# Pooled scores in two banks, local outputs by column halves, and small products in the gaps behind the first tile

## The chip, the core and the metric

One core of a Trainium2 chip runs the whole program. The engines are TensorE (PE; its weight loads are listed apart as PEld), VectorE (DVE), ScalarE (ACT), GpSimd (POOL) and SyncE (SP), which issues transfers. Each works through its own instructions in order, and semaphores tie them together. The metric is the device time of one execution in microseconds; lower is better. TensorE has two clock levels, 1.2 and 2.4 GHz; the profile gives the granted clock as a share of the upper one, so that 0.50 is the lower.

## What is computed

An attention layer over 4 batches, 8 heads, 576 positions and 64 dimensions, then two feed-forward layers on its 2304 tokens of 512 features. The attention has two branches that are added: one on positions pooled by four, and one in which each query sees only keys less than four positions away.

```python
q_d = q.reshape(B, H, Sd, factor, D).mean(axis=3)      # factor 4; k_d, v_d alike
out_up = np.repeat(sm_attn(q_d, k_d, v_d), factor, axis=2)
mask = np.abs(pos[:, None] - pos[None, :]) < factor
scores = np.where(mask, scale * np.matmul(q, k.transpose(0, 1, 3, 2)), -1000000000.0)
out_local = np.matmul(softmax(scores), v)
x = (out_up + out_local)                               # as [2304, 512]
h = x @ w_in;  x = (h * sigmoid(h)) @ w_out            # first layer, hidden size 2048
h = x @ w_in2; out = elu(h) @ w_out2                   # second layer
```

(softmax stands for the lines with the maximum, the exponential and the sum.)

## The kernel before

The 16 pairs of a batch and two heads are the units of the attention; the two heads of a pair lie in the two halves of 64 partitions. The first layer starts long before the attention is done: its tokens are cut into tiles of 256, its hidden features into tiles of 128, and `unit(n, f)` makes, for token tile n and hidden tile f, the first product (L1160, 12 matmuls, 128x256), the activation (ACT L1188, DVE L1189, ACT L1191, POOL L1194) and the second product (L1208, 12 matmuls). Each number of a product is split into a high and a low part and three of the four partial products are taken, so a weight tile has two parts too: DVE L466 and ACT L459 and L462 decode it, ACT L1137 rounds the high part, POOL L1141 makes the low part. From about 257 us on, the rest of the feed-forward work runs in another phase (`paired`, L1842 to L1999), which the change doesn't touch.

A pair passes PE in these steps: transposes of queries and keys (L674), local scores (L811: 20 matmuls of 64 columns on tiles of 64x64 of the array, for batch 0 with a mask product, L803, ahead), pooled scores (L884: six matmuls of 144 columns, `pooled_scores`, for three groups of pooled queries and two heads, the heads on the tiles at rows and columns 0 and 64), flips of the local weights (L928) and of the pooled weights (L950), pooled output (L975) and local outputs (L1041, `out_l`: 20 matmuls of about 57 columns, on four tiles of 64x64). Between the pooled scores and L950 stand the maximum (DVE L894), three exponentials (ACT L900), sums (DVE L908, L909) and a norm (POOL L915). L822 on POOL is the same norm for the local weights. L936 and L962 copy the flips from the banks.

PSUM is eight banks, `b0` to `b7`, handed out by `banks`: kind "h" for a first product's tile (it uses the left half of a bank), "y" for the second product's sums, "a" for the attention. A `Hold` is a bank that is taken when its first step is issued and given back after its last user.

The order of all engines' instructions up to about 257 us is made by a list scheduler while the program is built: every step is a `Job` with an engine, an assumed time, predecessors, holds and a due time. `pick` takes the job that can start earliest, and among those that can start within `SLACK` the one due first; on PE a job with the same tile size (`mode`) as the last one is preferred (`STICK`). So a changed number or hold moves the whole sequence. Until the first unit's first product is out (`FILL_TO`), `fill` puts products of a constant tile (L389, 512 columns) where the planner foresees that PE would stand still.

## Time and profile before

| | us |
| --- | --- |
| median of 3 runs | 859.21 |
| lowest, highest | 858.85, 860.39 |
| the profiled execution | 860.57 |
| its span in the profile | 858.8 |

| engine | busy us | share of the span |
| --- | --- | --- |
| PE | 849.1 | 99% |
| DVE | 679.0 | 79% |
| ACT | 566.9 | 66% |
| POOL | 197.2 | 23% |

The mean granted clock of PE is 0.996. The profile is of one execution. Matmuls are pipelined on PE, and the ends of their records are modelled, so the distance between the starts of two rows tells more than the duration in a row. A row of the timeline groups records of one line that follow each other; a matmul in fp32 shows as two records.

### The profile page before, as it was taken

The numbers are of one execution on the slowest core, as the hardware profiler recorded it, in microseconds if no ns is written. First come the engines' busy times: TensorE is split into PE (matmuls) and PEld (weight loads), VectorE is DVE, ScalarE is ACT, GpSimd is POOL, SyncE is SP. The second block draws the span as 40 slices with busy tenths as digits, with TensorE's granted clock in tenths as the row PEclk, the third lists the DMA queues.
The fourth block names the chain that finished last, engine by engine and source line by source line (L and its number), as shares of the span: only waits on it lengthen the run. The fifth ranks groups of instructions, "written<-read, shape, count | busy, mean of one in ns | idle before, by whom it ended". The sixth has DMA issues, their size and how long they took to land.

```text
span 858.8 us, 18415 instructions
## 1 busy us (share of the span) xinstructions
PE 849.1 (99%) x7032; PEld 817.6 (95%) x7032; DVE 679.0 (79%) x1360; ACT 566.9 (66%) x1316; POOL 197.2 (23%) x239
## 2 busy tenths in 40 slices
PE   9989999999999999999999999999999999999998
PEld 6878999999999999999999998899998999999997
DVE  6987776766947988967969889569889999487495
ACT  4877765655549876655478597377499885473662
POOL 6676785754000300000000111000020102002010
PEclk9989999999999999999999999999999999999999
DMA  9686977621065255033188466163586670561602
GB/s 174 167 191 172 179 187 192 154 65 78 27 168 178 81 195 160 1 129 93 64 243 286 168 238 229 65 230 105 188 285 221 209 268 15 199 207 38 229 29 74
DMA packets 120056, 132.66 MB, mean 154 GB/s; under 512 B 64992, under 2 KB 96224, under 8 KB 119840
## 3 DMA queue, kind: packets, MB, share of 16 engines
q1 hardware_dynamic: 117600, 130.90, 50.1%
q8 instruction: 55, 0.90, 0.5%
q10 hardware_dynamic: 2368, 0.59, 0.4%
q14 instruction: 33, 0.27, 0.1%
HBM read 89.26 MB, written 42.21 MB: 153 GB/s over the span
## 4 chain that ended last, share of the span: by engine, by line
PE 96%; DVE 2%; issue 1%; DMA 0%; ACT 0%; POOL 0%; DVEq 0%; SPq 0%; POOLq 0%
PE b L1894 34%; PE b L1844 14%; PE b L1208 8%; PE b L1997 8%; PE b L1999 8%; PE b L1160 7%; PE b L1842 7%; PE b L674 2%; PE b L884 1%; PE b L1041 1%; PE b L975 1%; PE b L811 1%; PE b L950 1%; PE b L928 1%; PE b L747 1%
## 5 line engine op out<-in xcount | busy, mean ns | idle before, releaser
L1160 PE MATMUL b<-xh,w 128*128 128x256 f32 x384 | 82.7, 296 | 0.0
L1208 PE MATMUL b<-gh,w 128*128 128x256 f32 x384 | 79.5, 289 | 0.0
L1894 PE MATMUL b<-xhr,xaw 128*128 128x384 f32 x288 | 77.3, 335 | 0.0
L1894 PE MATMUL b<-xhr,w 128*128 128x384 f32 x256 | 67.3, 334 | 0.0
L1160 PEld LDWEIGHTS b<-xh,w 128*128 128x128 f32 x384 | 64.8, 195 | 2.3 <-issue 1.4
L1208 PEld LDWEIGHTS b<-gh,w 128*128 128x128 f32 x384 | 62.9, 190 | 1.3 <-issue 0.8
L1906 ACT COPY hg<-b 128x384 f32<-128x384 f32 x60 | 28.9, 482 | 43.2 <-PE b L1894 42.8
L1804 DVE TENSOR_TENSOR part<-b,part 128x256 f32<-128x256 f32 (+3 forms) x91 | 41.1, 500 | 18.8 <-PE b L1844 17.8
L1902 DVE TENSOR_TENSOR b<-b,hg 128x384 f32<-128x384 f32 x60 | 33.5, 561 | 27.8 <-PE b L1894 17.2
L1208 PE MATMUL b<-gl,w 128*128 128x256 f32 x192 | 54.3, 283 | 0.0
L1894 PE MATMUL b<-xlr,xaw 128*128 128x384 f32 x160 | 53.5, 334 | 0.0
L1894 PEld LDWEIGHTS b<-xhr,xaw 128*128 128x128 f32 x288 | 52.4, 188 | 0.0
L1334 DVE TENSOR_TENSOR xlr<-tail,xhr 128x768 fp32r<-128x768 f32 x42 | 40.0, 954 | 14.8 <-ACT xhr L1331 14.6
L1160 PE MATMUL b<-xl,w 128*128 128x256 f32 x192 | 49.8, 286 | 0.0
L1997 PE MATMUL b<-grw,w 128*128 128x384 f32 x192 | 49.6, 334 | 0.0
L1894 PEld LDWEIGHTS b<-xhr,w 128*128 128x128 f32 x256 | 46.5, 188 | 0.0
L1331 ACT CAST xhr<-tail 128x768 fp32r<-128x768 f32 x42 | 35.5, 847 | 12.1 <-DVE tail L1506 11.2
L1894 PE MATMUL b<-xlr,w 128*128 128x384 f32 x128 | 42.8, 334 | 0.0
L1844 PE MATMUL b<-w,grw 128*128 128x256 f32 x228 | 42.6, 283 | 0.0
L1999 PE MATMUL b<-w,grw 128*128 128x512 f32 x132 | 41.6, 389 | 0.0
L822 POOL TENSOR_TENSOR ring<-ring,small 128x640 f32<-128x640 f32 x27 | 34.3, 1272 | 23.1 <-DVE small L854 14.1
L1333 POOL TENSOR_TENSOR ghk<-hg,grw 128x384 fp32r<-128x384 f32 x4 | 4.5, 1132 | 151.8 <-ACT grw L1331 151.8
(376 smaller groups left out, 2834.2 us busy)
## 6 DMA issues: line engine op xcount, KB each, us to landing
ws<-in_moe_w_in_dram SPq DMA_DIRECT2D x30, 512.0 KB, 5.5
ws<-in_moe_w_out_dram SPq DMA_DIRECT2D x30, 512.0 KB, 4.5
tailr<-xs SPq DMA_DIRECT2D x28, 384.0 KB, 4.3
xs<-xhr SPq DMA_DIRECT2D x21, 384.0 KB, 2.3
xs<-xlr SPq DMA_DIRECT2D x21, 384.0 KB, 2.8
x<-part SPq DMA_DIRECT2D x6, 768.0 KB, 3.8
tail<-x SPq DMA_DIRECT2D x12, 384.0 KB, 5.9
out_dram<-part SPq DMA_DIRECT2D x18, 256.0 KB, 2.0
```

Of the source, the lines that this page charges most:

```text
L822: eng.tensor_tensor(E3(s0, s1), E3(s0, s1), col3(h, s0, s1).to_broadcast([P, 2 * (s1 - s0), WIN]), op)
L1160: nc.tensor.matmul(ph.tile[:, :NB0], w[a][:, c, :], x_slot(n, c, b_), start=start and m == 0, stop=stop and m == len(products) - 1,)
L1208: nc.tensor.matmul(y[d // 2].tile[:, o:o + NB0], w[m // 2][:, sl], gg(m % 2), start=f == 0 and m == 0 and d % 2 == 0, stop=fin and m == 2, ...
L1331: a = Job("A", ACT_[width], lambda: nc.scalar.copy(hi(), at()), preds, gate)
L1334: other=("V", VEC_[width], lambda: nc.vector.tensor_tensor(lo(), at(), hi().bitcast(F32), ALU.subtract)),
L1804: nc.vector.tensor_tensor(dst, x, dst, ALU.add)
L1842: nc.tensor.matmul(y, wm[:, sl], gm, start=first, stop=last_, skip_group_check=True)
L1844: nc.tensor.matmul(y, gm[:, sl], wm, start=first, stop=last_, skip_group_check=True)
L1894: nc.tensor.matmul(acc_, a[:, cs], b[:, c, :], start=fresh and c == 0 and m == 0, stop=c == 1 and m == 2, skip_group_check=True,)
L1902: add = lambda out, x, y: Job("V", VEC_[NB], lambda: nc.vector.tensor_tensor(out, x, y, ALU.add), [], gate)
L1997: nc.tensor.matmul(y[d][:, :NB], wm[:, sl], gm, start=first, stop=last_)
L1999: nc.tensor.matmul(y[d], gm[:, sl], wm, start=first, stop=last_)
```

## The change

Three edits.

The pooled scores get two banks instead of one (`bankd`, `group_d`): groups 0 and 2 in the first, group 1 in the second. The six matmuls are issued so that the two heads' tiles write to the two banks in the first and third round. The maximum becomes two instructions, over two groups (288 elements) and one (144), the exponentials come in the order 0, 2, 1, and the planner's time for the block goes from 0.4 to 0.5.

The local outputs' 20 matmuls are issued in another order: first the ten whose results go to partitions 0 to 63 of the two banks, then the ten for partitions 64 to 127; within ten, the row halves and the banks take turns.

`fill_beside` goes on where `fill` ends, until the fourth hidden tile of the second token tile has its first product (`SOFT_TO`): where the planner foresees that PE would stand still by more than 0.3 us plus 0.115 us, it puts products of the mask tile (bf16, 256 columns, adding onto the unused right half of a bank that a first product holds). 25 such products come about.

```diff
--- before.py
+++ after.py
@@ -62,6 +62,7 @@
     POOL_G = 1
     D_ROWS, D_LOCAL, D_V, D_W, S_ROWS, S_LOCAL, X_AFTER = 1.6, 2.3, 1.75, 2.5, 1.1, 2.2, 1
     QUAD_FROM, MASK_PE = 0, 1
+    SOFT_TO = (1, FP // 2 - 1)
     FILL_TO, SAFE_R, SAFE_W = (0, 0), 0.0, 0.0
     LEND = 1
     SOON, W_EARLY, W_AT = 10.0, 0, -3.0
@@ -94,7 +95,7 @@
     QD = [a * SD // 3 for a in range(3)]
     QD_ROWS = (D, SD // 3)
     QD_FROM = ([min(a, SD - D) for a in QD], QD)
-    T_D = 0.4
+    T_D = 0.5
 
     LENT = {'rows': [(6, 0), (6, 1)], 'v': [(7, 1)]}
 
@@ -163,7 +164,7 @@
     now = [0.0]
     trim = [True]
     clock_of = {"A": 0.0, "V": 7.0, "G": 7.0, "S": 0.0, "P": 5.0, "dma": 0.0, "port": 7.0}
-    filling = [True]
+    filling, soft = [True], [True]
     serial = [0]
     mode_of = [None]
 
@@ -296,6 +297,8 @@
             if self.eng == "P":
                 if filling[0]:
                     fill(t)
+                elif soft[0]:
+                    fill_beside(t)
                 if self.mode != mode_of[0]:
                     dur += 0.12 if mode_of[0] is not None else 0.09
                 mode_of[0] = self.mode
@@ -392,6 +395,15 @@
         gap = t - clock_of["P"]
         filler(min(int((gap - 0.1) / 0.22), 40))
 
+    def fill_beside(t):
+        gap = t - clock_of["P"]
+        n = min(int((gap - 0.3) / 0.115), 40)
+        beside = [h for h in banks.busy.values() if h.kind == "h" and h.left > 0]
+        flat = masks.rearrange("p a s w -> p (a s w)")
+        if n > 0 and beside:
+            for _ in range(n):
+                nc.tensor.matmul(beside[0].tile[:, NB0:2 * NB0], flat[:, :P], flat[:, :NB0], start=False, stop=False, skip_group_check=True)
+
     wz = []
     fill_bank = Hold(banks, "f")
     fill_bank.left = 1
@@ -874,34 +886,41 @@
             )
 
 
-            bankd = Hold(banks, "a")
-
-            def pooled_scores(bankd=bankd):
+            bankd = [Hold(banks, "a") for _ in range(2)]
+
+            def group_d(a, bankd=bankd):
+                return bankd[a % 2].tile[:, a // 2 * SD:(a // 2 + 1) * SD]
+
+            def pooled_scores(group_d=group_d):
                 qD, kD = hqkD.tile, hqkD.tile[:, SD:]
-                for a in range(3):
-                    for j in range(2):
-                        c0, m = QD_FROM[j][a], D
-                        nc.tensor.matmul(
-                            bankd.tile[j * D:j * D + m, a * SD:(a + 1) * SD], qD[j * D:(j + 1) * D, c0:c0 + m], kD[j * D:(j + 1) * D, :],
-                            start=True, stop=True, skip_group_check=True,
-                        )
-
-            psd = follow(Job("P", T_D, pooled_scores, [red], lat=0.2, takes=[bankd, hsm] + [hED] * (b >= POOL_G), uses=[hqkD], mode="q"), "psd")
+                for j, a in ((0, 0), (1, 1), (0, 2), (1, 0), (0, 1), (1, 2)):
+                    c0 = QD_FROM[j][a]
+                    nc.tensor.matmul(
+                        group_d(a)[j * D:(j + 1) * D], qD[j * D:(j + 1) * D, c0:c0 + D], kD[j * D:(j + 1) * D, :],
+                        start=True, stop=True, skip_group_check=True,
+                    )
+
+            psd = follow(Job("P", T_D, pooled_scores, [red], lat=0.2, takes=bankd + [hsm] + [hED] * (b >= POOL_G), uses=[hqkD], mode="q"), "psd")
             hnm = Hold(NM)
             DP = D + QD_ROWS[1]
-            bank3d = lambda bankd=bankd: bankd.tile[:DP, :3 * SD].rearrange("p (a s) -> p a s", a=3)
-            nmj = Job(
-                "V", 0.14 + 0.00106 * SD * 3, lambda: nc.vector.tensor_reduce(hnm.tile[:DP, :3], bank3d(), axis=AX.X, op=ALU.max, negate=True),
-                [psd], takes=[hnm],
-            )
-
-            def exp_d():
-                for a in range(3):
+            nmj = []
+            for o in range(2):
+                na = 2 - o
+
+                def top_d(o=o, na=na, bankd=bankd):
+                    nc.vector.tensor_reduce(
+                        hnm.tile[:DP, o:3:2], bankd[o].tile[:DP, :na * SD].rearrange("p (a s) -> p a s", a=na), axis=AX.X, op=ALU.max, negate=True,
+                    )
+
+                nmj.append(Job("V", 0.14 + 0.00106 * SD * na, top_d, [psd] + nmj, takes=[] if o else [hnm]))
+
+            def exp_d(group_d=group_d):
+                for a in (0, 2, 1):
                     nc.scalar.activation(
-                        ED()[:DP, a, :], bank3d()[:, a, :], AF.Exp, bias=hnm.tile[:DP, a:a + 1], accum_out=hsm.tile[:DP, 2 * a:2 * a + 1],
+                        ED()[:DP, a, :], group_d(a)[:DP], AF.Exp, bias=hnm.tile[:DP, a:a + 1], accum_out=hsm.tile[:DP, 2 * a:2 * a + 1],
                     )
 
-            exps = [Job("A", 0.58 * 3, exp_d, [nmj], uses=[hnm, bankd])]
+            exps = [Job("A", 0.58 * 3, exp_d, nmj, uses=[hnm] + bankd)]
             mine = lambda: hnm.tile[:DP, :3]
 
             def invert():
@@ -1030,16 +1049,16 @@
 
             def out_l(banko=banko):
                 vw = hw.tile.rearrange("p (n d) -> p n d", d=D)
-                for i_ in range(NW // 2):
-                    for t in range(2):
-                        w = i_ + t * NW // 2
-                        n = a0[w + 1] - a0[w]
-                        c0 = (w % 2) * WIN + a0[w] - q0[w]
-                        o = a0[w] - t * HALF
-                        for j in range(2):
-                            p_ = (j + t) % 2 * D
+                for e in range(2):
+                    for i_ in range(NW // 2):
+                        for t in range(2):
+                            w = i_ + t * NW // 2
+                            n = a0[w + 1] - a0[w]
+                            c0 = (w % 2) * WIN + a0[w] - q0[w]
+                            o = a0[w] - t * HALF
+                            j = t ^ e
                             nc.tensor.matmul(
-                                banko[t].tile[p_:p_ + D, o:o + n],
+                                banko[t].tile[e * D:(e + 1) * D, o:o + n],
                                 vw[j * WIN:(j + 1) * WIN, w, :],
                                 aT()[j * WIN:(j + 1) * WIN, w // 2, c0:c0 + n],
                                 start=True, stop=True,
@@ -2083,6 +2102,8 @@
         run(g1_jobs[FILL_TO])
         filling[0] = False
         fill_bank.done(g1_jobs[FILL_TO][-1])
+        run(g1_jobs[SOFT_TO])
+        soft[0] = False
         run([j for b_ in range(B) for j in batch_end[b_]] + list(kept_x.values()) + [x for p_ in w_split.values() for x in p_])
         PREFER.clear()
         attn_pools.close()
```

Since the planner sees other times and holds, the order up to about 250 us is another one on all engines; from there on it is the same as before, row by row. Three places show it.

PE around the first unit's last products: `t` is the constant of the fill, `xh`, `xl` and `w` are the operands of the first product, `ident` that of the flips. Before:

```order
L389 MATMUL b_92<-t 128x512
L1160 MATMUL b_94<-xh,w_783 128x256
L1160 MATMUL b_94<-xl,w_783 128x256
L1160 MATMUL b_94<-xh,w_783 128x256
L950 MATMUL b_99<-ident,ring_120 72x112 x4
L950 MATMUL b_95<-ident,ring_120 72x112 x2
L975 MATMUL b_98<-ring_122,vd_142 64x144 x4
L1160 MATMUL b_93<-xh,w_931 128x256
```

After, where the first unit's last products end (the last two rows stand there 16 times in a row):

```order
L392 MATMUL b_92<-t 128x512
L1179 MATMUL b_98<-xh,w_844 128x256
L1179 MATMUL b_98<-xl,w_844 128x256
L1179 MATMUL b_98<-xh,w_844 128x256
L405 LDWEIGHTS mask
L405 MATMUL b_94<-mask 128x256
```

And after, nine products of the second hidden tile further on:

```order
L969 MATMUL b_97<-ident,ring_120 72x112 x4
L1179 MATMUL b_99<-xh,w_932 128x256
L1179 MATMUL b_99<-xl,w_932 128x256
L1179 MATMUL b_99<-xh,w_932 128x256
L969 MATMUL b_92<-ident,ring_120 72x112 x2
L1179 MATMUL b_99<-xh,w_932 128x256
```

Ahead of the second hidden tile's products (w_931, now w_932) stood the flips of the pooled weights and a pooled output; now the mask products stand there, and the flips come between the second tile's products.

POOL at the same place: L915 (now L934) is the norm of the pooled weights, L1141 (now L1160) the low part of a weight. Before:

```order
L822 TENSOR_TENSOR ring_119<-ring_119,small 128x640
L915 TENSOR_TENSOR ring_120<-ring_120,small 112x432
L1141 TENSOR_TENSOR w_888<-wf,w_888 128x512
L1141 TENSOR_TENSOR w_931<-wf,w_931 128x512
L1194 TENSOR_TENSOR gl<-t,gh 128x256
```

After:

```order
L778 TENSOR_TENSOR lent<-lent 72x2x128
L779 TENSOR_TENSOR vd_142<-lent 72x128
L1160 TENSOR_TENSOR w_932<-wf,w_932 128x512
L934 TENSOR_TENSOR ring_120<-ring_120,small 112x432
L834 TENSOR_TENSOR ring_119<-ring_119,small 128x640
L1160 TENSOR_TENSOR w_892<-wf,w_892 128x512
L1213 TENSOR_TENSOR gl<-t,gh 128x256
```

The second hidden tile's weight (w_931, now w_932) stood behind the norm and the first tile's second weight (w_888, now w_892); now it stands ahead of both.

PE in a block of local outputs of the same pair: `vw` are the values and `ring_121` the flipped weights; a row with x2 is one matmul on each of two tiles. Before, the end of the block:

```order
L1041 MATMUL b_96<-ring_121,vw_116 64x57 x2
L1041 MATMUL b_94<-ring_121,vw_116 64x56 x2
L1041 MATMUL b_96<-ring_121,vw_116 64x57 x2
L1041 MATMUL b_94<-ring_121,vw_116 64x61 x2
L1160 MATMUL b_99<-xh,w_998 128x256
```

After, the middle of the block, where the second column half begins with the row of 60 columns:

```order
L1060 MATMUL b_92<-ring_121,vw_116 64x57
L1060 MATMUL b_99<-ring_121,vw_116 64x56
L1060 MATMUL b_92<-ring_121,vw_116 64x57
L1060 MATMUL b_99<-ring_121,vw_116 64x61
L1060 MATMUL b_92<-ring_121,vw_116 64x60
L1060 MATMUL b_99<-ring_121,vw_116 64x57
```

Before, two tiles wrote to one bank and then the other two to the other, in turn; now single matmuls take turns between two banks, ten for one column half and then ten for the other.

## Rows read from the trace of the kernel before

**Rows 1.** The page, part 1: busy time, share of the span, instructions.

```profile
PE 849.1 (99%) x7032; PEld 817.6 (95%) x7032; DVE 679.0 (79%) x1360; ACT 566.9 (66%) x1316; POOL 197.2 (23%) x239
```

**Rows 2.** Windows of one microsecond: busy time of each engine, granted clock, DMA share, GB/s.

```profile
48.00:49.00 1.00, 1.00 (x9) 0.61 (x6) 1.00 (x1) 0.22 (x2) 1.00 (x2) 0.50 1.08 309
```

**Rows 3.** Waits of PE over the span: total us, times, longest us.

```profile
PE b L950 <- POOL ring L915: 2.2, 2, 2.1
```

**Rows 4.** Timeline of PE: start us, us, engine, line, operation, tiles, count, [idle before].

```profile
46.21 0.80 PE L950 MATMUL b<-ident,ring 112*72 112x112 f32 x6 [2.05 <-POOL ring L915]
47.60 1.23 PE L975 MATMUL b<-ring,vd 72*64 72x144 f32 x8 [0.59 <-ACT ring L962]
48.76 0.58 PE L1160 MATMUL b<-xh,w 128*128 128x256 f32 x1
...
52.13 0.84 PE L928 MATMUL b<-ident,ring 128*128 128x128 f32 x3
...
53.83 0.62 PE L674 MATMUL b<-ident,nat 96*128 96x96 f32 x5
...
65.17 0.28 PE L1160 MATMUL b<-xl,w 128*128 128x256 f32 x1
...
69.54 0.55 PE L928 MATMUL b<-ident,ring 128*128 128x128 f32 x3 [0.51 <-POOL ring L822]
...
70.42 0.36 PE L1160 MATMUL b<-xh,w 128*128 128x256 f32 x1
...
71.19 0.71 PE L975 MATMUL b<-ring,vd 72*64 72x144 f32 x8 [0.18 <-DVE t L1189]
71.84 0.39 PE L1160 MATMUL b<-xh,w 128*128 128x256 f32 x1
```

**Rows 5.** Timeline of the engines that feed PE, the same stretch.

```profile
44.98 1.17 POOL L915 TENSOR_TENSOR ring<-ring,small 112x432 f32<-112x432 f32 x1 [0.86 <-DVE small L909]
...
46.12 2.50 POOL L1141 TENSOR_TENSOR w<-wf,w 128x512 fp32r<-128x512 f32 x2
...
53.01 0.48 ACT L936 COPY ring<-b 128x384 f32<-128x384 f32 x1 [1.28 <-PE b L928]
...
54.08 1.29 POOL L1141 TENSOR_TENSOR w<-wf,w 128x512 fp32r<-128x512 f32 x1 [2.41 <-ACT w L1137]
```

**Rows 6.** Timeline of PE: local scores beside small blocks, and between products.

```profile
22.39 0.75 PE L811 MATMUL b<-xa 64*64 64x64 f32 x40
22.97 0.65 PE L884 MATMUL b<-xb 64*64 64x144 f32 x7
...
59.34 0.28 PE L1160 MATMUL b<-xh,w 128*128 128x256 f32 x1
59.55 0.81 PE L811 MATMUL b<-tail 64*64 64x64 f32 x40
60.29 0.39 PE L1208 MATMUL b<-gh,w 128*128 128x256 f32 x1
60.51 0.28 PE L1208 MATMUL b<-gl,w 128*128 128x256 f32 x1
```

**Rows 7.** Timeline of PE: pooled scores beside the mask, and between products.

```profile
11.96 0.70 PE L884 MATMUL b<-xb 64*64 64x144 f32 x7
12.38 0.32 PE L803 MATMUL b<-mask,unit 64*64 64x320 bf16 x1
...
62.28 0.95 PE L884 MATMUL b<-qkD 64*64 64x144 f32 x12
63.16 0.38 PE L1160 MATMUL b<-xh,w 128*128 128x256 f32 x1
```

**Rows 8.** Timeline of PE: local outputs between products.

```profile
55.83 0.81 PE L1041 MATMUL b<-ring,vw 64*64 64x60 f32 x40
56.57 0.38 PE L1160 MATMUL b<-xh,w 128*128 128x256 f32 x1
```

**Rows 9.** Groups of 10 to 257 us: busy us, mean ns, idle before.

```profile
L894 DVE TENSOR_REDUCE small<-b 112x3 f32<-112x432 f32 x16 | 9.7, 604 | 2.9 <-PE b L884 2.8
```

## The prediction

> **What bounds the kernel now.** I read the page first: TensorE (PE) is busy in 99% of the span [rows 1]. So nothing but PE's own time, and the few places where PE stands still, can move the end. The waits of PE come next: in the stretch that the change re-orders there is one long one, the transposes of the pooled weights waiting for GpSimd (POOL) [rows 3]. In the timeline it lies before 46.21 us and lasts 2.05 us; 0.59 us more follow before 47.60 [rows 4]. The windows of one microsecond show what follows these idles: from 48 to 49 the granted clock is 0.50, the 1.2 GHz level, where it is 1.00 in most of the span [rows 2]. After 71 us the timeline of PE is a dense stream, so what is won or lost on PE inside that stream reaches the end, and a stall that is removed reaches it only if the engines that feed PE are early enough.
>
> **The early gap and the clock.** The fill puts 16 small products where PE stood still, behind the first unit of the first layer (9 more stand later). Its cover is exactly that gap; if PE did not stand still there, 16 products at the 0.12 us of a step would cost up to 1.9 us. What a kept clock is worth is read from the same work at both levels [rows 4, 7]: a block of 16 steps of the first product takes 48.76 to 52.13, 3.37 us, and 63.16 to 65.17, 2.01 us, at full clock (1.36 won); the flips with three steps between them take 52.13 to 53.83, 1.70, against 69.54 to 70.42, 0.88 (0.82 won); the pooled output takes 47.60 to 48.76, 1.16, against 71.19 to 71.84, 0.65 (0.51 won). Together 2.7 us for the clock, and 2.05 + 0.59 = 2.6 us for the gaps, 5.3 us at most.
>
> Not all of that can be had. The weight of the second hidden tile leaves POOL at 46.12 + 2.50 = 48.62 [rows 5], 0.14 us before PE uses it at 48.76: with the gap filled and nothing else moved PE would have stood still for the weight instead. The change moves that weight on POOL ahead of the norm of the pooled scores and of the first tile's second weight, which is worth about 2.4 us there (1.17 for the norm, half of 2.50 for the weight [rows 5]), so PE should not wait for it. Behind it the chain is tight: POOL idles 2.41 us before 54.08 for ACT's cast, and ACT idles 1.28 before 53.01 for the flips on the slow PE [rows 5]. Those idles vanish with a fast PE, but they are about as long as the clock's 2.7 us and not as the 5.3. I therefore count the clock's share and leave the gaps' share to the feeding engines: **−2.7 us**, bounds −5.3 and 0.
>
> **Pooled scores in two banks.** Six products as before, two row-and-column tiles as before, only the bank differs. If the tiles had run one after the other, 12 records of 144 columns would need twelve steps. The pooled output gives a step: 0.65 us less 0.16 of boundary (below) for 8 records in four pairs is 0.122 us a pair, all of it from one set of rows. The pooled scores take 62.28 to 63.16, 0.88 less 0.15, for six pairs: 0.122 again [rows 4, 7]. And at 12.38, while the passes that began at 11.96 still run, a mask product begins on another tile [rows 7]. So the two tiles already run side by side in one bank: **0**. The Trainium skill says otherwise: "TensorEngine Tiling (Array Packing)", section "Gotcha 1: PSUM Pressure", states that different row tiles cannot access one PSUM bank at the same time. By that rule the new order, which meets the same bank in one of three slots instead of all, would gain; the sum would then be 2.9 us lower. The measured 0.122 us speaks against it; what it would make of the time is the third rival.
>
> The maximum on VectorE (DVE) becomes two instructions for one of 0.604 us [rows 9]; the elements stay the same, so DVE pays between nothing and another 0.6 us per pair, and, as it walks no element twice, I take it near nothing. The exponentials on ACT wait for both maxima, as they waited for the one, so no gain can come of it. The second bank is one fewer for the products' tiles, which the planner knows. All of it lies beside PE's stream, and I count **0**, bounds 0 and +2 (0.17 us of waiting in each of 12 pairs, a third of the 0.51 that PE waits before 69.54 for POOL [rows 4]).
>
> **Local outputs.** This block has 20 matmuls of 57 columns, 40 records. Before, all four tiles come in turn: 55.83 to 56.57 is 0.74 us between products, less 0.16 of boundary is 0.58 for ten rounds of four, 0.058 a round [rows 8]. After, the first ten matmuls use only the two tiles of one column half and the next ten the two of the other. Two tiles with ten records each need 0.58 us, and the other half needs 0.58 more. It is +0.58 if the second half waits for the first, and 0 if it overlaps it entirely. What PE overlaps shows at 11.96: six passes of 0.122 run there, and the mask product on other tiles, the next in order, begins at 12.38, in the fourth pass [rows 7]. So PE sees about three passes ahead, no further. Of ten passes the second half would then begin after six to seven; I take six, 6 × 0.058 = 0.35 us per block. From the first unit on, 12 pairs have such a block, all in PE's dense stream: 12 × 0.35 = **+4.2 us**, bounds 0 and 12 × 0.58 = +7.0.
>
> **Fewer changes of tile size.** The new order strings blocks of 64-wide tiles together more often. The price of a boundary: the block of local scores takes 59.55 to 60.29, 0.74 us, between products, but 22.39 to 22.97, 0.58, beside other small blocks; the step before it is 59.34 to 59.55, 0.21 where 0.12 is usual, and the step behind it 60.29 to 60.51, 0.22 [rows 6]. That is 0.16 + 0.09 + 0.10 = 0.35 us for a way in and a way out. Counted along PE's two orders from the first unit on, there are 32 ways in and out before and 25 after: 7 × 0.35 = **−2.4 us**, bounds −2.5 and −1.1, the latter if only the 0.16 of the block itself is saved (the changes from one small block to another rise from 15 to 21, and may cost something).
>
> **The sum.** −2.7 + 0 + 0 + 4.2 − 2.4 = −0.9 us. The profiled execution took 860.57 us (span 858.8); 859.7 would follow. The median of the runs is 859.21, 1.36 below the profiled one, and I carry the difference over: 859.21 − 0.9 = **858.3 us**. About 0.2%, 1.7 us, is what a measurement of this kernel can tell from no change; so this forecast counts as no change, leaning faster.
>
> **Rivals.** First, slower: the local outputs decide. If PE doesn't look into the second column half before the first is through, each block costs 0.58 instead of 0.35: 12 × 0.23 = 2.8 us more, 861.1. It holds from a lookahead of none; for it speaks that 20 records are queued on two tiles, against it the mask product at 12.38 [rows 7].
>
> Second, faster: the feeding engines keep up, and the gaps are won along with the clock: 2.6 us more, 855.7. For it speaks the weight moved ahead on POOL by 2.4 us, against it that the idles to be won back [rows 5] are no longer than 2.4.
>
> Third, faster: sharing a bank slows both tiles of the pooled scores. Then of six half-speed slots a third stay, and 0.735 us becomes 0.49: 12 × 0.245 = 2.9 us less, 855.4. The pooled output's equal step, without sharing between rows, speaks against it [rows 4, 7].
>
> Fourth, slower, and the change not doing what it says: the fill misses. If the second weight or another feeder comes late, PE stands still at another place, or the clock falls there, and the early term is 0: 858.3 + 2.7 = 861.0. For it speaks how tight the chain of weights is [rows 5]; the later fill has the same weakness.
>
> **How the numbers follow.** Forecast 0.36, first rival 0.20, second 0.16, third 0.10, fourth 0.18. The forecast's own spread (the boundaries' price, a pass more or less of lookahead at 0.7 us) is 856.8 to 860.4. Below 857.5 lie the second and third and a quarter of the forecast: 0.35. Above 860.9 lie most of the first and fourth: 0.31. Between: 0.34. The range that reaches the rivals and the bounds of the small terms, leaving out only two of them at once on one side (864 or 853), is 854.3 to 862.6.
>
> **What would show it.** Right: no gap of PE and a granted clock of 1.00 from 44 to 55; a block of pooled scores still 0.88 us between products; local outputs at 1.05 to 1.1 instead of 0.74 there; the first-layer stream starting its later tiles 2 to 3 us earlier around 75 us, and losing half of it until 250. Wrong: pooled scores near 0.64 (third rival), local outputs at 1.3 (first) or still 0.74 (then 4 us faster than forecast), a granted clock of 0.50 anywhere behind 40 us (fourth), or waits of PE for ACT or POOL beyond 0.5 us in a place that has none now.

## The result and the profile after

The changed kernel takes 866.67 us (median of 4 runs, 865.75 to 868.47), the kernel before 859.22. The ratio is 1.0089, its 95% interval 1.0072 to 1.0105: slower by 7.4 us, where 858.3 was forecast with 862.6 as the upper end. In the profiled executions the span goes from 858.8 to 865.4, by 6.6 us.

The page of the changed kernel, the line of the span and part 1 (busy time, share, instructions), beside [rows 1]:

```profile
span 865.4 us, 18468 instructions
...
PE 855.5 (99%) x7059; PEld 825.6 (95%) x7059; DVE 679.1 (78%) x1372; ACT 565.5 (65%) x1319; POOL 199.3 (23%) x239
```

PE is busy 6.4 us longer, and its share is the same 99%. So the loss is PE's own time again, and the waits are as short in sum as before. But they stand elsewhere. The longest wait of PE in the changed kernel (total us, times, longest), beside [rows 3]:

```profile
PE b L994 <- ACT ring L981: 2.8, 1, 2.8
```

The long wait for the norm (2.2 us, [rows 3]) is gone, and a wait of the pooled output (L994, L975 before) for its copied flips has come, 2.8 us. (Flips are transposes; their results are copied out of PSUM before the output can use them.) The timeline of PE (start, us, engine, line, operation, tiles, count, idle before) shows both ends of the change:

```profile
46.19 0.29 PE L1179 MATMUL b<-xh,w 128*128 128x256 f32 x1
46.32 1.92 PE L405 MATMUL b<-mask 128*128 128x256 bf16 x16
47.99 0.36 PE L1179 MATMUL b<-xh,w 128*128 128x256 f32 x1
...
51.16 0.49 PE L947 MATMUL b<-ident,ring 128*128 128x128 f32 x3
54.49 1.23 PE L994 MATMUL b<-ring,vd 72*64 72x144 f32 x8 [2.84 <-ACT ring L981]
```

The 16 products of the mask do fill the old gap, and the second weight's products follow without a stop at 47.99. PE then runs out at 51.65 and stands still until 54.49. The row at 46.19 is the last product step ahead of the old gap, the 18th of the first products. Before, it stands at

```profile
43.88 0.28 PE L1160 MATMUL b<-xh,w 128*128 128x256 f32 x1
```

Up to this step both kernels have done the same work, the fill apart: the same numbers of products, of transposes and flips, of scores and of outputs, among them four blocks of local outputs. So the changed kernel is 2.3 us late before the first product of the mask. Lines have moved: L1179 is L1160 of before, L994 is L975, L947 is L928, L1060 is L1041, L898 is L884. The windows of one microsecond (busy time of PE, PEld, DVE, ACT, POOL, granted clock, DMA share, GB/s), beside [rows 2]:

```profile
52.00:53.00 1.00, 0.00 (x0) 0.00 (x0) 1.00 (x2) 0.00 (x0) 1.00 (x2) 1.00 0.00 0
53.00:54.00 1.00, 0.00 (x0) 0.00 (x0) 0.52 (x2) 0.92 (x2) 0.64 (x1) 0.88 0.00 0
54.00:55.00 1.00, 0.51 (x4) 0.51 (x6) 0.25 (x1) 1.00 (x4) 0.00 (x0) 0.50 0.57 86
...
59.00:60.00 1.00, 1.00 (x9) 0.89 (x8) 0.54 (x2) 0.00 (x0) 1.00 (x2) 0.50 1.18 198
```

The clock falls with the new wait as it fell with the old one: 1.00 while PE stands still from 52 to 53, 0.88 from 53 to 54, 0.50 from 54 to 60. Why the copies come late is read from the engines that make them, in the same view of all engines:

```profile
49.17 3.88 DVE L478 SCALAR_TENSOR_TENSOR wf<-ws,wf 128x512 int32<-128x512 int32 x1
...
49.33 1.26 POOL L834 TENSOR_TENSOR ring<-ring,small 128x640 f32<-128x640 f32 x1
...
50.55 1.28 POOL L1160 TENSOR_TENSOR w<-wf,w 128x512 fp32r<-128x512 f32 x1
...
51.78 0.72 POOL L1213 TENSOR_TENSOR gl<-t,gh 128x256 fp32r<-128x256 f32 x1
52.46 1.18 POOL L1125 TENSOR_TENSOR xl<-xa,xh 128x256 fp32r<-128x256 f32 x1
52.98 0.54 DVE L982 COPY ring<-b 72x384 f32<-72x384 f32 x1
...
53.09 0.62 ACT L1156 CAST w<-wf 128x512 fp32r<-128x512 f32 x1 [2.53 <-DVE wf L478]
...
53.61 0.62 ACT L474 ACTIVATE wf<-wf 128x512 int32<-128x512 int16 x1
54.14 0.29 ACT L981 COPY ring<-b 72x192 f32<-72x192 f32 x1
```

VectorE's weight step (L478) takes 3.88 us. All that time GpSimd works without a gap, four instructions from 49.33 on. Behind the step waits one copy of the flips on VectorE (L982, 52.98). ScalarE waits for the step too, 2.53 us, with the cast of that weight (L1156), and the other copy (L981, 54.14) stands behind it.

The two blocks that the change rewrites, where they stand between products, beside [rows 7] and [rows 8]:

```profile
67.32 0.95 PE L898 MATMUL b<-qkD 64*64 64x144 f32 x12
68.20 0.38 PE L1179 MATMUL b<-xh,w 128*128 128x256 f32 x1
...
77.05 1.20 PE L1060 MATMUL b<-ring,vw 64*64 64x60 f32 x40
78.18 0.38 PE L1179 MATMUL b<-xh,w 128*128 128x256 f32 x1
```

The pooled scores take 0.88 us, exactly as before. The local outputs take 1.13 us where they took 0.74.

To see what part of the loss lies where, I added up the distances from start to start in both traces, each counted to the row that it leads to, from 80 us to the same place of the next phase (the 60th step there). This needs no model: 181.99 us before, 188.51 after. After has 36 more product steps and 7 more transposes left at 80 us, which take **4.6 us**: that much is lost before 80, and 2.3 of it ahead of the old gap, as the row at 46.19 shows. In the rest, the ten blocks of local outputs take 11.50 us instead of 7.98, **+3.5**; the pooled scores, flips and pooled outputs together 2.3 less and the local scores 0.6 more, **−1.7**. That is 6.4 of the 6.5 us.

### The profile page after: what moved, and what is told of

The parts are those of the page before. It is cut to its first block, busy times and chain, and to the rows that moved or that the text cites. A ratio compares the mean times of both kernels' runs of the same rounds, so it can differ in the third digit from the quotient of the medians.

```text
span 865.4 us, 18468 instructions
## 1 busy us (share of the span) xinstructions
PE 855.5 (99%) x7059; PEld 825.6 (95%) x7059; DVE 679.1 (78%) x1372; ACT 565.5 (65%) x1319; POOL 199.3 (23%) x239
## 4 chain that ended last, share of the span: by engine, by line
PE 95%; DVE 2%; POOL 1%; DMA 0%; issue 0%; ACT 0%; DVEq 0%; SPq 0%; POOLq 0%
PE b L1913 34%; PE b L1863 14%; PE b L1227 8%; PE b L2016 8%; PE b L2018 8%; PE b L1179 7%; PE b L1861 7%; PE b L1060 2%; PE b L686 2%; PE b L994 1%; PE b L898 1%; PE b L823 1%; PE b L947 1%; PE b L969 1%; PE b L759 1%; DVE wf L478 1%
## 5 line engine op out<-in xcount | busy, mean ns | idle before, releaser
L1179 PE MATMUL b<-xh,w 128*128 128x256 f32 x384 | 81.1, 292 | 0.1
L1179 PEld LDWEIGHTS b<-xh,w 128*128 128x128 f32 x384 | 63.4, 191 | 1.6 <-issue 0.4
L1179 PE MATMUL b<-xl,w 128*128 128x256 f32 x192 | 49.0, 282 | 0.0
L1350 ACT CAST xhr<-tail 128x768 fp32r<-128x768 f32 x42 | 35.5, 848 | 11.6 <-DVE tail L1525 11.5
L478 DVE SCALAR_TENSOR_TENSOR raw<-ws,raw 128x512 int32<-128x512 int32 x48 | 32.7, 683 | 7.9 <-ACT raw L474 7.8
```

Of the source, the lines that this page charges most:

```text
L478: nc.vector.scalar_tensor_tensor(out(), st[:, :, 0], 13, out(), op0=ALU.logical_shift_right, op1=ALU.bitwise_or)
L1179: nc.tensor.matmul(ph.tile[:, :NB0], w[a][:, c, :], x_slot(n, c, b_), start=start and m == 0, stop=stop and m == len(products) - 1,)
L1350: a = Job("A", ACT_[width], lambda: nc.scalar.copy(hi(), at()), preds, gate)
```

## The experiments

Theory A: the local outputs' new order costs its own time, and the new order of all engines brings a wait as long as the old. Rival B: the two banks, or the extra products, cost by themselves. Every ratio below is to the kernel before on the same chip. Its median there was 859.62 us for the first four experiments, 859.51 for the two banks alone, the four tiles in turn, the copies on ScalarE alone and the planner's 0.4, and 860.67 for the other four; times from different chips are compared by these ratios.

**The old output order in the changed kernel.** The loop of `out_l` as it was:

```diff
-                for e in range(2):
-                    for i_ in range(NW // 2):
...
+                for i_ in range(NW // 2):
...
+                        for j in range(2):
+                            p_ = (j + t) % 2 * D
```

> The changed kernel with the local outputs' loop as it was before; the two banks, the fill and the planner's order stay. Theory A (the local outputs' new order costs its own time): the trace of the changed kernel has 1.13 us from the start of a block to the next step between products where before had 0.74, and all 16 blocks sum to 19.6 us instead of 12.7; so 5.5 to 7 us come back, 859.7 to 861.2 us, and a block is 0.74 again. Rival B (the planner's other order of the whole first part is what costs, with the wait of 2.8 us before 54.5): at most 2.5 us come back, 864 us or more.

Measured: 862.75 us, ratio 1.0035 (1.0020 to 1.0051). 3.9 us come back (4.6 by the ratios, 1.0089 and 1.0035): theory A's direction, but less than the 5.5 that it asked for, and 3 us of loss stay. The blocks are 0.74 us again. In the profiled execution the pooled output waited 3.5 us instead of 2.8, and that took some of it back.

**The changed kernel without the extra products.**

```diff
-    filling, soft = [True], [True]
+    filling, soft = [True], [False]
```

> The changed kernel without the 25 products of the mask; all else stays, the order too. Theory A: the 16 products behind the first unit stand where PE would wait for the second weight anyway, and the wait of 2.8 us before 54.5 stays, so only the 9 later ones (1.1 us) and a part of the 16 come back: 864.8 to 866.2 us. Rival B (the fill is pure extra work, since the gap went elsewhere): all of their 2.85 us comes back, 863.8 us or less. If they keep the clock up, it is slower than the changed kernel.

Measured: 866.60 us, 1.0080 (1.0066 to 1.0094). Nothing comes back, just above the range of theory A. The timeline of PE in that run says why, with the idle time in brackets:

```profile
48.84 0.39 PE L1179 MATMUL b<-xh,w 128*128 128x256 f32 x1 [0.51 <-ACT w L1156]
...
50.19 0.51 PE L1179 MATMUL b<-xh,w 128*128 128x256 f32 x2 [0.85 <-POOL w L1160]
...
56.36 0.71 PE L994 MATMUL b<-ring,vd 72*64 72x144 f32 x8 [2.83 <-ACT ring L981]
```

Without the products PE waits for the second weight, 0.51 us for its high part and 0.85 for its low part, and for the flips as before. The fill stood in front of waits, and taking it away gives those waits back.

**The new output order alone, in the kernel before.**

```diff
-                for i_ in range(NW // 2):
...
+                for e in range(2):
+                    for i_ in range(NW // 2):
...
+                            j = t ^ e
```

> The kernel before with the local outputs' new order alone. Theory A: 0.39 us for each of 16 blocks, of which those of the first pairs may be hidden in the fill before the first unit: 863.9 to 865.7 us. Rival B: less than 2 us over before, 861.2 us or less.

Measured: 864.06 us, 1.0050 (1.0037 to 1.0063): 4.4 us more, theory A. One thing in its profile was not expected. The waits in the timeline of PE, and the windows of ten microseconds:

```profile
48.03 0.80 PE L950 MATMUL b<-ident,ring 112*72 112x112 f32 x6 [1.89 <-POOL ring L915]
49.42 0.71 PE L975 MATMUL b<-ring,vd 72*64 72x144 f32 x8 [0.59 <-ACT ring L962]
```

```profile
40.00:50.00 10.00, 7.46 (x97) 5.86 (x96) 9.61 (x19) 8.81 (x24) 7.87 (x9) 1.00 0.77 160
50.00:60.00 10.00, 10.00 (x150) 9.40 (x147) 8.54 (x10) 7.90 (x19) 8.72 (x10) 1.00 0.78 193
```

PE waits 1.89 and 0.59 us, near the 2.05 and 0.59 of [rows 4], and the clock stays at 1.00. So the fall of the clock does not follow from such a wait each time, and where it stays away, it hides a part of what the local outputs cost. The last product step ahead of the gap starts at 45.87 here, 2.0 us later than before, with four blocks of local outputs ahead of it; at 80 us this kernel has the same work left as the kernel before, and the ten blocks behind 80 us take 11.79 us for 7.98.

**The extra products alone, in the kernel before.** `fill_beside` and its hooks, nothing else; the order of all other instructions is that of before.

```diff
                 if filling[0]:
                     fill(t)
+                elif soft[0]:
+                    fill_beside(t)
```

> The kernel before with the products of the mask alone; the order of all other instructions is that of before, and the planner puts 18 of them into the gap before the flips at 46.2 us and 4 more around the steps behind it. Theory A (with the gap of before filled and no new one behind it the clock stays up): the granted clock is 1.00 from 44 to 55 and 1.5 to 3 us are won, 856.2 to 857.7 us. Rival B (a filled gap wins nothing, the weights that come late set the pace): 858.5 to 860.5 us, with PE waiting for a weight between 46 and 57 us.

Measured: 858.45 us, 0.9985 (0.9974 to 0.9997). The windows:

```profile
40.00:50.00 10.00, 9.58 (x80) 8.12 (x82) 9.82 (x15) 7.87 (x22) 9.07 (x10) 1.00 0.73 167
50.00:60.00 10.00, 10.00 (x155) 9.20 (x154) 8.75 (x16) 8.84 (x21) 7.93 (x8) 1.00 1.01 231
```

The gap is filled, the clock is 1.00 in both windows, as theory A said. Of the 5.3 us that gap and clock together are worth at most, 1.2 us arrive, 0.15%: less than the 1.5 of theory A, and next to what rival B gave for the time, though not by its waits.

**The two banks alone, in the kernel before.** The matmuls, maxima and exponentials as in the change; the order of the engines is then that of the changed kernel.

```diff
-    T_D = 0.4
+    T_D = 0.5
...
-            bankd = Hold(banks, "a")
+            bankd = [Hold(banks, "a") for _ in range(2)]
```

> The kernel before with the two banks for the pooled scores alone (and the planner's 0.5 for 0.4); the order of all engines' instructions is then that of the changed kernel, without the products of the mask and with the local outputs in the old order. Theory A (the other order makes the pooled output wait for its copied flips, by some 2.8 to 3.5 us, and that is a new price of the edit): 861.5 to 863.5 us, with one such wait between 50 and 56 us. Rival B (the two banks cost nothing, the 3 us that the changed kernel keeps with the old output order are the fill's 2.85): 859 to 860.5 us.

Measured: 862.04 us, 1.0033 (1.0020 to 1.0047). Theory A. The two longest waits of PE at this place, in its timeline:

```profile
48.38 0.51 PE L1167 MATMUL b<-xh,w 128*128 128x256 f32 x2 [1.20 <-POOL w L1148]
...
55.00 1.23 PE L982 MATMUL b<-ring,vd 72*64 72x144 f32 x8 [3.50 <-ACT ring L969]
```

The wait for the copies is there without the fill and without the new output order. It belongs to the order that the planner made from this edit. The last product step ahead of the old gap is late here too, at 46.05. From 80 us on this run shows the good side of that order too: pooled scores 1.0 us less, flips and pooled outputs 1.0 less, local outputs 0.8 less, local scores 0.6 more, in sum 2.1 us won. I put that down to fewer changes of tile size; the part of the second bank in it is not tested by itself.

**All four tiles in turn, with row halves and banks still in turn.**

```diff
-                for e in range(2):
-                    for i_ in range(NW // 2):
+                for i_ in range(NW // 2):
+                    for e in range(2):
```

> The changed kernel with the local outputs' two outer loops exchanged: row halves and banks still take turns from one matmul to the next, but the column half changes after every second one, so that all four tiles are in turn. Theory A (what costs is that only two tiles have work at a time): the block is 0.74 us between products again and the time is that of the changed kernel with the old output order, 862 to 863.5 us. Rival B (the order of banks and row halves is what counts): it stays at 1.1 us a block and 866 us or more.

Measured: 864.49 us (five runs, 860.66 to 865.77), 1.0049 (1.0028 to 1.0069). The block, between products:

```profile
78.89 0.81 PE L1060 MATMUL b<-ring,vw 64*64 64x60 f32 x40
79.63 0.39 PE L1179 MATMUL b<-xh,w 128*128 128x256 f32 x1
```

0.74 us: the block is as short as before, so what costs is that only two tiles have work, and the order of banks and row halves is worth nothing. The time is above the 862 to 863.5 of theory A, and the interval overlaps that of the first experiment. The profiled execution (864.59 us) has a loss that is not the block's: PE stood still for 2.60 us before 37.45, waiting for nothing that the profile shows, and the clock was 0.50 from 39 to 42. Whether the four others had such a stand is not known.

**Short stretches of a column half, in the kernel before.**

```diff
-                for e in range(2):
-                    for i_ in range(NW // 2):
+                for lo, hi, e in ((0, 2, 0), (0, 2, 1), (2, 4, 0), (2, 4, 1), (4, 5, 0), (4, 5, 1)):
+                    for i_ in range(lo, hi):
```

> The kernel before with the local outputs by column halves in short stretches: four matmuls of one half, four of the other, and so on, so that each tile has four passes in a row and not ten. Theory A (PE looks three passes ahead and takes up the other half's matmuls then): a block is 0.74 to 0.85 us between products, and the time 859 to 861 us. Rival B (each change of the column half costs by itself; there are five of them instead of one): a block is 1.2 us or more and the time above 864.1 us, that of the kernel before with ten of each half.

Measured: 861.12 us, 1.0000 (0.9989 to 1.0011): no change, though 0.1 us above the range of theory A. The block (a pass is one record of a matmul on its tile):

```profile
72.74 0.85 PE L1041 MATMUL b<-ring,vw 64*64 64x60 f32 x40
73.52 0.38 PE L1160 MATMUL b<-xh,w 128*128 128x256 f32 x1
```

0.78 us with five changes of the half, against 1.13 with one. So a change costs next to nothing, and PE takes up work for other tiles a few passes ahead: four passes in a row are covered, ten are not. From 0.39 us and 0.058 a pass the uncovered part of ten is 6.7 passes, which leaves about three: an estimate from this block alone.

**The copies of the pooled flips on ScalarE alone,** in the changed kernel with the old output order:

```diff
-                flips_d.append(alike(
...
+                flips_d.append(Job("A", 0.19 + 0.0008 * n, lambda dst=dst, src=src: nc.scalar.copy(dst(), src()), [pj], uses=[bank]))
```

> The changed kernel with the old output order, and with the copies of the pooled flips on ScalarE alone (they may go to either engine otherwise); the planner's order follows. In the run with the old output order the pooled output waited 3.5 us for such a copy, whose one half stood on VectorE behind a weight step that took several microseconds instead of 0.7, and whose other half stood on ScalarE behind the weight's cast that waits for that step. Theory A (that placement is the new price): the wait of the pooled output falls below 1 us and 1.5 to 3 us come back, 859.8 to 861.3 us. Rival B (late weights set the pace of this stretch whatever stands where): another wait takes its place and the time stays at 862 to 863.5 us.

Measured: 857.97 us, 0.9980 (0.9967 to 0.9993): 4.8 us less than with the old output order alone, more than theory A gave. The planner's order follows the edit, so not all of it need be the copies'. VectorE and ScalarE at that place:

```profile
52.33 4.92 DVE L478 SCALAR_TENSOR_TENSOR wf<-ws,wf 128x512 int32<-128x512 int32 x2 [1.15 <-ACT wf L474]
```

```profile
51.30 0.47 ACT L980 COPY ring<-b 72x384 f32<-72x384 f32 x1
...
52.20 0.30 ACT L980 COPY ring<-b 72x192 f32<-72x192 f32 x1
...
56.13 0.62 ACT L1152 CAST w<-wf 128x512 fp32r<-128x512 f32 x1 [1.94 <-DVE wf L478]
```

The weight steps are as slow as ever, 4.92 us for two. But both copies now stand ahead of the cast that waits for them (1.94 us, 56.13), and nothing of it reaches PE; the clock is 1.00 from 40 to 70.

**One norm of GpSimd left out,** in the changed kernel with the old output order:

```diff
             def across(eng, h, op, s0=s0, s1=s1):
+                if i == 4 and eng is nc.gpsimd and op == ALU.mult:
+                    return
```

> The changed kernel with the old output order, and with one norm of GpSimd left out (the local weights of batch 1, first head pair, are not divided by their sums); all engines' order is else the same. The norm took 1.26 us at 49.3 us, at the head of a row of GpSimd instructions without a gap, beside which VectorE's weight step took 3.9 us instead of 0.7. Theory A (the weight step gets on only once GpSimd has a gap, and the late copy and the wait of PE follow from it): the step becomes 1 to 1.5 us shorter, and so does the wait of the pooled output, 861 to 862 us. Rival B (the step is long for another reason): it stays at 3.9 us and the time at 862.5 us or more.

Measured: 860.04 us (857.65 to 863.40), 0.9995 (0.9982 to 1.0009): 0.4% less than with the norm by the ratios, about 3.4 us, and below the 861 to 862 of theory A. VectorE and GpSimd with the norm, then without:

```profile
48.79 4.70 DVE L478 SCALAR_TENSOR_TENSOR wf<-ws,wf 128x512 int32<-128x512 int32 x1
53.42 0.54 DVE L982 COPY ring<-b 72x384 f32<-72x384 f32 x1
```

```profile
49.08 1.26 POOL L834 TENSOR_TENSOR ring<-ring,small 128x640 f32<-128x640 f32 x1
...
52.23 0.72 POOL L1125 TENSOR_TENSOR xl<-xa,xh 128x256 fp32r<-128x256 f32 x1
57.78 1.28 POOL L1160 TENSOR_TENSOR w<-wf,w 128x512 fp32r<-128x512 f32 x1 [4.84 <-ACT w L1156]
```

```profile
48.87 3.50 DVE L478 SCALAR_TENSOR_TENSOR wf<-ws,wf 128x512 int32<-128x512 int32 x1
52.29 0.54 DVE L984 COPY ring<-b 72x384 f32<-72x384 f32 x1
```

```profile
51.09 0.72 POOL L1127 TENSOR_TENSOR xl<-xa,xh 128x256 fp32r<-128x256 f32 x1
56.26 1.27 POOL L1162 TENSOR_TENSOR w<-wf,w 128x512 fp32r<-128x512 f32 x1 [4.44 <-ACT w L1158]
```

and the pooled output on PE without it:

```profile
53.80 0.83 PE L996 MATMUL b<-ring,vd 72*64 72x144 f32 x8 [2.31 <-ACT ring L983]
```

With the norm GpSimd's row ends at 52.23 + 0.72 = 52.95 and the weight step at 53.49; without it at 51.81 and 52.37. The step ends 0.55 us behind the row both times, 1.1 us earlier without the norm, and the pooled output's wait falls from 3.50 to 2.31. Theory A for the step: it gets on once GpSimd pauses. The wait explains 1.2 us of the gain; the rest is open. The GPSIMD Engine Reference of the Trainium skill, "1. Specifications", says that GpSimd shares its SBUF interfaces with VectorE, with contention for VectorE instructions that read two inputs from SBUF; this step reads two, and the trace agrees.

**The planner's 0.4 in place of 0.5,** in the changed kernel with the old output order:

```diff
-    T_D = 0.5
+    T_D = 0.4
```

> The changed kernel with the old output order and the planner's time for the pooled scores at 0.4 as before, instead of 0.5. The work is the same, the order another one. Theory A (the price hangs on the order that the planner happens to find, not on the two banks): the time differs from 862.75 us by over 1 us, and in this order no cast of a weight stands between the two copies of the first layer's flips, so it is below, 859 to 861.5 us. Rival B (the two banks cost by themselves, by the second maximum or by the bank that the products lack): 862 to 863.5 us again.

Measured: 858.71 us, 0.9987 (0.9978 to 0.9997). 4 us less with the same work, a little below the 859 to 861.5 of theory A: with the two banks the kernel need not be slower than before, and the loss of 3 us hangs on the order. Whether the banks cost something that this order makes up for is not shown.

**The 0.4 and the copies on ScalarE together,** two of the edits above in one kernel:

```diff
-    T_D = 0.5
+    T_D = 0.4
...
-                flips_d.append(alike(
...
+                flips_d.append(Job("A", 0.19 + 0.0008 * n, lambda dst=dst, src=src: nc.scalar.copy(dst(), src()), [pj], uses=[bank]))
```

> The changed kernel with the old output order, the planner's 0.4 for the pooled scores, and the copies of the pooled flips on ScalarE alone: the two edits that each brought the kernel below the time of before, together. Theory A (each avoids the same late copy): no more than either alone, 857 to 859 us. Rival B (their gains add up): 855 to 857 us.

Measured: 860.13 us, 0.9994 (0.9985 to 1.0003). The gains don't add up; by the ratio it is less than either alone, and the time is above theory A's 857 to 859. Its planner's order has another wait of PE, 1.4 us, for a step of the local scores on VectorE.

**The extra products and the copies on ScalarE alone, in the kernel before,** pooled scores in one bank and local outputs in the old order:

```diff
+                elif soft[0]:
+                    fill_beside(t)
...
-                flips_d.append(alike(
...
+                flips_d.append(Job("A", 0.19 + 0.0008 * n, lambda dst=dst, src=src: nc.scalar.copy(dst(), src()), [pj], uses=[bank]))
```

> The kernel before with the products of the mask and with the copies of the pooled flips on ScalarE alone; pooled scores in one bank. If the two banks bring something by themselves once the late copy is gone, this is slower than 857.97 us, the same with two banks; if they bring nothing, it is 857 to 858.5 us. The order is the planner's, so a difference of 1 us says little about the banks.

Measured: 855.04 us, 0.9940 (0.9928 to 0.9952), the fastest of all and faster than both kernels. Its windows, beside those of the extra products alone:

```profile
40.00:50.00 10.00, 9.55 (x81) 8.01 (x78) 9.79 (x16) 7.90 (x22) 9.07 (x10) 1.00 0.72 166
50.00:60.00 10.00, 10.00 (x156) 9.22 (x155) 8.73 (x15) 9.05 (x21) 7.92 (x8) 1.00 0.94 212
```

The clock is 1.00 here as well, and PE is as busy. It is 0.45% below the extra products alone by the ratios (3.4 us by the medians), and below the expected 857 to 858.5. PE's longest wait between 40 and 260 us is 0.5 us. Which part of its order brings this I did not take apart. With one bank it is faster than the run with two and the copies on ScalarE (0.9980), so nothing here shows a gain of the second bank.

## Why the prediction was wrong

**The early gap and the clock: −2.7 predicted, and this is the step that failed, together with the stretch ahead of it, which the prediction put at nothing.** At 80 us the changed kernel is 4.6 us behind.

The first half of that, 2.3 us, is lost before the gap (46.19 against 43.88). The prediction counted local outputs and changes of tile size only "from the first unit on" and gave no reason why the new order of all engines should cost nothing before. The output order alone is 2.0 us late at that step (45.87), the two banks alone 2.2 (46.05), the changed kernel with the old output order 2.1 (45.96). So each of the two edits brings it and together they bring no more; what makes it stays open. These are single traces, but they agree: with the engines' order of before and local outputs of 0.74 or 0.78 us the step stands at 43.88, 42.47 (the extra products alone) and 44.37 (the short stretches), with the changed kernel's order at 45.96 or later in all six.

The second half is lost at the gap. The prediction followed the second weight on GpSimd and found it early enough, and there it was right: PE went on at 47.99. It did not follow the copies of the flips. In the kernel before both were on ScalarE, at 46.86; in the new order one stands on VectorE behind a weight step, the other on ScalarE behind the cast that needs that step. Such a step could be seen to last long in the trace of before:

```profile
46.83 5.39 DVE L466 SCALAR_TENSOR_TENSOR wf<-ws,wf 128x512 int32<-128x512 int32 x2
46.86 0.69 ACT L962 COPY ring<-b 72x384 f32<-72x384 f32 x2
```

Two steps took 5.39 us beside a busy GpSimd, and I had read it only as a limit of the weights. So the old wait of 2.05 + 0.59 us became one of 2.84, the clock fell just the same, and the fill (25 products, 2.8 us of PE's time from start to start) paid for waits on a weight and not for the wait that mattered. One block of local outputs came to lie in the slow stretch and took 1.95 us (57.28 to 59.23).

The fourth rival had this ("PE stands still at another place, or the clock falls there") with a chance of 0.18, but priced it at a gain of 0 (861.0 us), as if a new wait could be no worse than no gain. With the first part re-ordered, the fill paid and the clock lost again, it was a loss.

The size of the term was too large as well. With the old order and the gap filled, the clock stayed up and 1.2 us came of it, where 2.7 were counted. A slip in the reading of the rows works the other way: the slow block of the first product (48.76 to 52.13) has 15 steps and not 16, so the clock's price was 2.8 and not 2.7.

**Local outputs: right in kind and size per block.** 0.35 us predicted, 0.35 measured over the ten blocks behind 80 us, 0.39 between products. By itself the edit costs 4.4 us in the kernel before and 3.9 in the changed one, against 4.2 predicted. That the 4.4 comes so near is partly luck: 2.0 us of cost ahead of the first unit, which the 4.2 leave out, and a clock that stayed up about cancel by 80 us in its trace. The first rival (0.58) was wrong: PE does look ahead some three passes, as the mask product at 12.38 showed [rows 7].

**Pooled scores: right.** The block is 0.88 us in two banks as in one. The third rival, by which sharing a bank slows both tiles, fell, and with it the rule that the prediction cites beside it, for the time of these blocks: no run shows a conflict of row tiles in one bank.

**Changes of tile size: near in size.** −2.4 predicted for the whole; −1.7 is what the other small blocks take less behind 80 us in the changed kernel, and −2.1 with the local outputs in the run with the two banks alone. That the changes of tile size make it is argued, not tested.

**The two maxima and the second bank: 0 predicted.** The 0.4 for 0.5 shows a kernel that has them and is no slower than before (858.71 us). On VectorE the two maxima take 11.5 us for 16 pairs where one took 9.7 [rows 9]. What they do to the planner's order is another matter: in the run with the two banks alone 4.0 us are lost before 80 us, 2.2 of them ahead of the old gap, and 2.1 won behind it.

From 80 us on the sum was then +1.8 us, against +1.1 by its terms (ten blocks at 0.35 less 2.4). Nearly all of the miss lies before: 4.6 us lost instead of about 2 won.

## What to carry to other kernels

Where an edit lets a scheduler re-order several engines, follow not only the wait that is to vanish but each producer of the next steps on the stalled engine, and what stands ahead of it on its own engine: a copy of half a microsecond behind a slow step is a new stall. Count the stretch ahead of the place that the edit is aimed at too: half of the early loss was there. Work placed on a tile array wants all tiles in turn at distances of a few passes; ten passes for two tiles and then ten for the others took 1.13 us a block here instead of 0.74. An edit that is free in one order of the schedule can cost 4 us in another, so it is tried with several.

## What the runs showed of the hardware

VectorE's weight step of 0.7 us lasted up to 4.7 us beside a GpSimd without a pause, and ended 0.55 us behind GpSimd's row both with and without the norm. The two steps of the kernel before ended so too, at 52.22 behind a row that ended at 51.67. In the changed kernel's own profile it ended at 53.05, within the last instruction of the row, which took 1.18 us there instead of 0.72. The granted clock fell to 0.50 with waits of 2.05 and 0.59 us in the kernel before and with one of 2.84 us in the changed one, and stayed at 1.00 behind 1.89 and 0.59 us in the run with the new output order alone; what decides between them is open.
